# ScalarE's order written out for the whole kernel, and two roundings per block pair moved from ScalarE to GpSimd

## The chip, the core and the metric

The kernel runs on one core of a Trainium2 chip. The metric is the device time of one execution in microseconds. Five engines work side by side, each through its own queue in order: TensorE (PE in the profile, its weight loads PEld), VectorE (DVE), ScalarE (ACT), GpSimd (POOL) and SyncE (SP), which here only issues transfers. They wait for each other through semaphores.

## The reference

Two parts, one after the other. First an attention through 49 agents, for 4 batches of 12480 rows of 128 numbers:

```python
a2k = sm(agents, k)          # softmax over the 12480 rows of k
agent_v = a2k @ v            # 49 x 128 per batch
q2a = sm(q, agents)          # softmax over 49, for each row of q
x = q2a @ agent_v
h = x @ w_in                 # 128 -> 2048
out = (h - tanh(h)) @ w_out  # 2048 -> 128
```

`sm` scales by 1/sqrt(128), subtracts the maximum, exponentiates and divides by the sum. All is fp32, and `w_in` and `w_out` come as 64-bit floats that the kernel decodes.

## The kernel before

`agent_v @ w_in` is computed once per batch (49 x 2048), so that h comes straight from p, the softmax of q. Most products are made from fp32 numbers split in two, a rounded high part (fp32r) and the low rest; the two parts of p lie one above the other on 98 partitions, and the 49 x 2048 matrix is kept twice to match.

The main loop works on blocks of 500 columns (25 per batch, 100 in all). A block has 8 steps of 256 of the 2048 hidden units; two blocks make a pair of 16 steps (`pos` 0 to 15), and there are 50 pairs, 800 steps. For a step k the chain is:

- TensorE: h = two halves x two parts, four matmuls (`m1`, L544 and L545), into one of three PSUM buffers.
- ScalarE: y = tanh(c h) (L554), then z = y squared (L556). Both have two buffers. h times z is, up to a factor, h - tanh(h) for the small h that occur.
- VectorE: g = h z (`mul`, L562).
- GpSimd (or ScalarE): gh = g rounded (`high`, L595 on GpSimd, L593 on ScalarE).
- VectorE: gl = g - gh (`low`, L600).
- TensorE: six matmuls into the output block (`m2`): four with gh (L612, L613), two with gl (L615). One step in 16, and all of block 0, uses plain fp32 instead (L609) and has no gh or gl.

In iteration k of the loop TensorE makes h of step k+2 and then the output matmuls of step k-1; VectorE makes g of step k and then gl of step k-1; ScalarE makes y and z of step k+1.

Between these stand jobs, generators that advance by one stage in each iteration (`live`): the softmax of the next pair's q (`q_softmax`, begun at position 2: scores on TensorE L495, maximum on VectorE L502, a copy out of PSUM on ScalarE L503, the subtraction of the maximum on GpSimd L506, the exponential L510, sum and division L512 to L515, the rounded part of p on ScalarE L518, the low part on GpSimd L521); transposes of p and their copies (L531, L536); the copy of a finished output block (`finish`, o, L776). During the first three batches there is also work for the next batch: scores with k (three groups per pair, L278, L280, L286), then value products (three per pair, begun at positions 1, 3 and 12: subtraction on GpSimd L322, exponential L329, matmuls L337, sum L349), then the projection with `w_in` (L458 to L472).

What sets the order: on VectorE, GpSimd and TensorE each instruction has an ordering link to the one before it in program order (`issue_order`, L873 to L875). On ScalarE that holds only up to the eighth step (L860). After that a scheduler places ScalarE's instructions, with one rule: jobs of an iteration come behind the square of the iteration before (L840). `wait_for` (L635) adds a real wait: from the third pair on, the q subtraction and the low part of p wait until the latest `mul` is done. `QGAPS` says how many iterations lie between the stages of `q_softmax`; `QACT` names the two positions (4 and 9) whose rounding ScalarE does; in iterations that begin a value product ScalarE rounds too.

## Time and profile before

| | |
|---|---|
| three runs | 2145.88, 2146.28, 2146.33 us; median 2146.28 |
| profiled execution | 2144.79 us, span 2143.0 us, mean granted TensorE clock 0.997 |
| first and last product g | begin 59.0 us, end 2133.2 us |
| TensorE, VectorE, ScalarE, GpSimd busy | 2085.6, 1960.8, 1918.9, 1312.3 us |
| roundings on GpSimd, on ScalarE | 608, mean 1744 ns; 135, mean 1026 ns |
| VectorE's product waits for ScalarE's square | 134.7 us in 177 places |

A row of a timeline reads: start in us from the span's beginning, duration, engine, line, operation, what is written <- what is read, shapes, count; in brackets the engine's idle time before it and what ended that. TensorE's matmuls are pipelined and their ends modelled: one of 500 columns shows 0.39 us, while the next begins after about 0.23. A busy share near 100% therefore hides short stalls.

### The profile page before, as it was taken

To read this page: it belongs to the slowest core of one execution; us is meant where nothing else is said; L and a number is where in the kernel's file an instruction comes from. 1 tells how busy PE (TensorE), PEld (TensorE's weight loads), DVE (VectorE), ACT (ScalarE), POOL (GpSimd) and SP (SyncE) were. 2 spreads that over 40 slices of the span, in tenths; PEclk is the share of its full clock that TensorE was granted. 3 is DMA by queue.
4 is the path that set the end of the run, shared out by engine and by line. 5 is a ranking of instruction groups with operands and counts; after the bars stand their busy time and mean duration, and the time that the engine had idled before them with its cause. 6 is when DMAs were issued, how large, how long until landed. Compare 5 with 4: busy or idle time off the path is not lost.

```text
span 2143.0 us, 37562 instructions
## 1 busy us (share of the span) xinstructions
PE 2085.6 (97%) x14885; PEld 1632.7 (76%) x14885; DVE 1960.8 (91%) x2028; ACT 1918.9 (90%) x2232; POOL 1312.3 (61%) x761
## 2 busy tenths in 40 slices
PE   8999999999999999999999999999999999999998
PEld 7577777777777777777777777777777877777776
DVE  7899898989998999888999989998999999999998
ACT  3888899899998889989998889988999999999997
POOL 0465675556656665565666566655566766767666
PEclk9999999999999999999999999999999999999999
DMA  9222112210111111112002210121010010000000
GB/s 352 76 79 70 42 39 70 61 50 30 39 50 50 62 59 50 50 51 68 20 20 69 69 33 20 52 66 42 20 40 20 20 39 20 30 29 20 29 11 21
DMA packets 65353, 109.17 MB, mean 51 GB/s; under 512 B 3984, under 2 KB 44176, under 8 KB 65168
## 3 DMA queue, kind: packets, MB, share of 16 engines
q1 hardware_dynamic: 65168, 106.68, 15.2%
q8 instruction: 119, 1.95, 0.4%
q14 instruction: 66, 0.54, 0.1%
HBM read 81.10 MB, written 25.56 MB: 50 GB/s over the span
## 4 chain that ended last, share of the span: by engine, by line
PE 69%; DVE 16%; ACT 8%; issue 5%; DMA 1%; POOL 0%; SPq 0%; ACTq 0%; POOLq 0%; DVEq 0%
PE h L544 14%; PE misc L615 13%; PE h L545 13%; PE misc L612 11%; PE misc L613 11%; DVE gl L600 7%; DVE g L562 5%; ACT z L556 4%; PE misc L609 3%; ACT y L554 2%; PE misc L337 2%; PE misc L278 1%; PE misc L531 1%; PE h L250 1%; PE misc L495 1%
## 5 line engine op out<-in xcount | busy, mean ns | idle before, releaser
L595 POOL TENSOR_SCALAR gh<-g 128x1000 fp32r<-128x1000 f32 (+1 forms) x608 | 1060.6, 1744 | 663.9 <-DVE g L562 609.1
L562 DVE TENSOR_TENSOR g<-h,z 128x1000 f32<-128x1000 f32 (+1 forms) x800 | 951.8, 1192 | 144.4 <-ACT z L556 134.7
L600 DVE TENSOR_TENSOR gl<-g,gh 128x1000 fp32r<-128x1000 f32 (+1 forms) x743 | 906.4, 1220 | 9.5 <-ACT gh L593 4.8
L554 ACT ACTIVATE y<-h 128x1000 f32<-128x1000 f32 (+1 forms) x800 | 801.6, 1002 | 106.2 <-PE h L545 101.2
L556 ACT ACTIVATE z<-y 128x1000 f32<-128x1000 f32 (+1 forms) x800 | 828.0, 1040 | 19.5 <-DVE g L562 0.6
L544 PE MATMUL h<-pT,awh 98*128 98x500 f32 (+1 forms) x1600 | 670.2, 419 | 2.6 <-ACT awh L461 1.4
L545 PE MATMUL h<-pT,awl 98*128 98x500 f32 (+1 forms) x1600 | 622.4, 389 | 0.2 <-DVE awl L464 0.2
L612 PE MATMUL misc<-gh,wo_l 128*128 128x500 f32 (+1 forms) x1486 | 576.1, 388 | 0.5 <-POOL gh L595 0.3
L613 PE MATMUL misc<-gh,wo_h 128*128 128x500 f32 (+1 forms) x1486 | 575.6, 387 | 0.0
L615 PE MATMUL misc<-gl,wo_h 128*128 128x500 f32 (+1 forms) x1486 | 469.1, 397 | 37.6 <-DVE gl L600 35.6
L615 PEld LDWEIGHTS misc<-gl,wo_h 128*128 128x128 f32 x1486 | 265.8, 188 | 133.2 <-DVE gl L600 87.6
L544 PEld LDWEIGHTS h<-pT,awh 98*128 98x128 f32 x1600 | 300.7, 188 | 85.5 <-issue 15.2
L545 PEld LDWEIGHTS h<-pT,awl 98*128 98x128 f32 x1600 | 302.7, 189 | 65.9 <-issue 14.4
L612 PEld LDWEIGHTS misc<-gh,wo_l 128*128 128x128 f32 x1486 | 279.6, 188 | 57.9 <-POOL gh L595 1.9
L613 PEld LDWEIGHTS misc<-gh,wo_h 128*128 128x128 f32 x1486 | 280.7, 189 | 56.0
L593 ACT CAST gh<-g 128x1000 fp32r<-128x1000 f32 (+1 forms) x135 | 138.6, 1026 | 0.0
L506 POOL TENSOR_TENSOR qe<-qe,qm 126x392 f32<-126x392 f32 x50 | 81.6, 1631 | 83.5 <-ACT qe L503 42.3
L521 POOL TENSOR_TENSOR pp<-qe,pp 126x392 fp32r<-126x392 f32 x50 | 94.2, 1885 | 24.4 <-ACT pp L518 7.5
L322 POOL TENSOR_TENSOR s<-s,mb 128x392 f32<-128x392 f32 (+1 forms) x39 | 70.2, 1800 | 50.5 <-DVE g L562 50.5
L609 PE MATMUL misc<-g,wo_f 128*128 128x500 f32 (+1 forms) x196 | 90.1, 581 | 0.0
L536 ACT CAST pT<-misc 98x500 fp32r<-98x500 f32 (+1 forms) x100 | 56.1, 562 | 14.2 <-PE misc L531 14.2
L776 ACT ACTIVATE o<-misc 128x500 f32<-128x500 f32 (+1 forms) x100 | 57.2, 572 | 5.1 <-PE misc L615 5.1
(104 smaller groups left out, 838.3 us busy)
## 6 DMA issues: line engine op xcount, KB each, us to landing
kt<-kT SPq DMA_DIRECT2D x48, 512.0 KB, 3.8
qt<-qT SPq DMA_DIRECT2D x46, 500.0 KB, 3.6
outT<-o SPq DMA_DIRECT2D x46, 500.0 KB, 2.6
v<-v SPq DMA_DIRECT2D x36, 512.0 KB, 4.0
vt<-v SPq DMA_DIRECT2D x12, 512.0 KB, 7.5
raw<-w_in SPq DMA_DIRECT2D x4, 512.0 KB, 9.2
v<-w_out SPq DMA_DIRECT2D x4, 512.0 KB, 9.0
qt<-qT SPq DMA_DIRECT2D x4, 490.0 KB, 3.4
```

Of the source, the lines that this page charges most:

```text
L544: nc.tensor.matmul(h[:, c, :w], aw[0][:A2, sl], pT[:A2, :w], start=True, stop=False)
L545: nc.tensor.matmul(h[:, c, :w], aw[1][:A2, sl], pT[:A2, :w], start=False, stop=True)
L554: nc.scalar.activation(self.pair(y), h, AF.Tanh, scale=TSC)
L556: nc.scalar.activation(z, y, AF.Square)
L562: self.nc.vector.tensor_tensor(self.pair(g), h, self.pair(z), ALU.mult)
L593: self.nc.scalar.copy(gh, g)
L595: self.nc.gpsimd.tensor_scalar(gh, g, 1.0, 0.0, ALU.mult, ALU.add)
L600: self.nc.vector.tensor_tensor(gl, g, gh.bitcast(F32), ALU.subtract)
L609: nc.tensor.matmul(acc[:, :w], wf[:, c * C : (c + 1) * C], gh[:, x], start=f == 0, stop=f == NCH - 1)
L612: nc.tensor.matmul(acc[:, :w], self.wo_l[:, f, :], gh[:, x], start=f == 0, stop=False)
L613: nc.tensor.matmul(acc[:, :w], self.wo_h[:, f, :], gh[:, x], start=False, stop=False)
L615: nc.tensor.matmul(acc[:, :w], self.wo_h[:, f, :], gl[:, x], start=False, stop=f == NCH - 1)
```

## The change

- The constants: `QACT` is gone, `QGAPS` becomes (1, 1, 0, 2, 2, 1, 1). The q subtraction now comes in the same iteration as the copy before it (position 4 rather than 5), the exponential at position 6 rather than 7; sum and division stay at 8, the rounded p at 9, its low part at 10.
- The two waits for the latest `mul` in `q_softmax` are gone. That of the value product (L322) stays.
- `pre` is split in `tanh` and `square`. Iteration k now emits, for ScalarE: the tanh of step k+1, the jobs, a rounding if one is due, the square of step k+1.
- The roundings of positions 4 and 9 go to GpSimd. Only those of iterations that begin a value product stay on ScalarE, and they are emitted one iteration later, just ahead of the next square.
- ScalarE's order is fixed by links from end to end, as on the other engines.

The matmuls' order on TensorE and the transfers' on SyncE do not move, and VectorE's moves in one place only. No arithmetic is changed.

On ScalarE, around positions 8 to 11 of a pair with k scores, there stood before (o is the finished output block, s the scores, pp the split p, y, z, g, gh as above; numbers tell buffers apart):

```order
L518 CAST pp_2886<-qe_2703 126x8x49
L286 COPY s_1009<-misc_2813 128x392
L554 ACTIVATE y_2893<-h_2871 128x1000
L593 CAST gh_2899<-g_2897 128x1000
L556 ACTIVATE z_2895<-y_2893 128x1000
L776 ACTIVATE o_2910<-misc_2618 128x500
L554 ACTIVATE y_2918<-h_2888 128x1000
L554 ACTIVATE y_2939<-h_2913 128x1000
L556 ACTIVATE z_2920<-y_2918 128x1000
L556 ACTIVATE z_2941<-y_2939 128x1000
```

and now:

```order
L285 COPY s_1011<-misc_2815 128x392
L551 ACTIVATE z_2873<-y_2865 128x1000
L546 ACTIVATE y_2886<-h_2875 128x1000
L514 CAST pp_2888<-qe_2705 126x8x49
L551 ACTIVATE z_2890<-y_2886 128x1000
L546 ACTIVATE y_2910<-h_2892 128x1000
L770 ACTIVATE o_2912<-misc_2618 128x500
L551 ACTIVATE z_2915<-y_2910 128x1000
L546 ACTIVATE y_2934<-h_2917 128x1000
L551 ACTIVATE z_2936<-y_2934 128x1000
```

The rounding gh has left, the two tanh in a row have become one tanh and one square in turn, and the copies of s, p and o stand between a tanh and its square.

On GpSimd, in the same pair, from the rounding of position 3 on, before:

```order
L595 TENSOR_SCALAR gh_2692<-g_2690 128x1000
L506 TENSOR_TENSOR qe_2703<-qe_2703,qm_2702 126x392
L595 TENSOR_SCALAR gh_2776<-g_2774 128x1000
L595 TENSOR_SCALAR gh_2799<-g_2797 128x1000
L595 TENSOR_SCALAR gh_2882<-g_2880 128x1000
L521 TENSOR_TENSOR pp_2886<-qe_2703,pp_2886 126x8x49
L595 TENSOR_SCALAR gh_2924<-g_2922 128x1000
```

and now:

```order
L589 TENSOR_SCALAR gh_2692<-g_2690 128x1000
L504 TENSOR_TENSOR qe_2705<-qe_2705,qm_2704 126x392
L589 TENSOR_SCALAR gh_2719<-g_2717 128x1000
L589 TENSOR_SCALAR gh_2776<-g_2774 128x1000
L589 TENSOR_SCALAR gh_2800<-g_2798 128x1000
L589 TENSOR_SCALAR gh_2882<-g_2880 128x1000
L589 TENSOR_SCALAR gh_2899<-g_2897 128x1000
L516 TENSOR_TENSOR pp_2888<-qe_2705,pp_2888 126x8x49
L589 TENSOR_SCALAR gh_2924<-g_2922 128x1000
```

The rounding of position 4 (gh_2719) has come behind the q subtraction, that of position 9 (gh_2899) ahead of the low part of p.

On ScalarE, positions 3 to 6 of a pair with value products, before:

```order
L329 ACTIVATE s_1009<-s_1009 128x392
L593 CAST gh_4035<-g_4033 128x1000
L554 ACTIVATE y_4058<-h_4024 128x1000
L503 COPY qe_4049<-misc_3991 126x392
L556 ACTIVATE z_4060<-y_4058 128x1000
L554 ACTIVATE y_4089<-h_4053 128x1000
L593 CAST gh_4064<-g_4062 128x1000
L556 ACTIVATE z_4091<-y_4089 128x1000
L329 ACTIVATE s_1009<-s_1009 128x392
L554 ACTIVATE y_4112<-h_4084 128x1000
L556 ACTIVATE z_4114<-y_4112 128x1000
L510 ACTIVATE qe_4049<-qe_4049 126x392
```

and now:

```order
L546 ACTIVATE y_4045<-h_4028 128x1000
L328 ACTIVATE s_1011<-s_1011 128x392
L502 COPY qe_4049<-misc_3993 126x392
L587 CAST gh_4054<-g_4033 128x1000
L551 ACTIVATE z_4056<-y_4045 128x1000
L546 ACTIVATE y_4075<-h_4058 128x1000
L551 ACTIVATE z_4086<-y_4075 128x1000
L546 ACTIVATE y_4105<-h_4088 128x1000
L506 ACTIVATE qe_4049<-qe_4049 126x392
L328 ACTIVATE s_1011<-s_1011 128x392
L551 ACTIVATE z_4110<-y_4105 128x1000
```

The rounding of position 3 (of g_4033) has gone behind the next tanh, the exponential and the q copy; that of position 4 (gh_4064) has left; and the two exponentials of position 6 stand together ahead of a square.

```diff
-QGAPS = (1, 1, 1, 2, 1, 1, 1)
-QACT = (4, 9)
+QGAPS = (1, 1, 0, 2, 2, 1, 1)
...
         yield from (None,) * gaps[2]
-        first = self.count()
         nc.gpsimd.tensor_tensor(ev, ev, m[:TT, :, None].broadcast_to([TT, GT, A]), ALU.subtract)
-        if gaps != (1,) * 7:
-            self.wait_for(first, self.mul_at)
...
-        first = self.count()
         nc.gpsimd.tensor_tensor(pp[:TT, :, A:], ev, pp[:TT, :, :A].bitcast(F32), ALU.subtract)
-        if gaps != (1,) * 7:
-            self.wait_for(first, self.mul_at)
...
-    def pre(self, h, w):
-        nc = self.nc
+    def tanh(self, h, w):
         y = self.wtile("y", NB["y"])[:, : 2 * w]
-        nc.scalar.activation(self.pair(y), h, AF.Tanh, scale=TSC)
-        z = self.wtile("z", NB["z"])[:, : 2 * w]
-        nc.scalar.activation(z, y, AF.Square)
-        self.act_at = self.last_name()
+        self.nc.scalar.activation(self.pair(y), h, AF.Tanh, scale=TSC)
+        return y
+
+    def square(self, y):
+        z = self.wtile("z", NB["z"])[:, : y.shape[1]]
+        self.nc.scalar.activation(z, y, AF.Square)
         return z
...
+        def tanhs(k):
+            if k < len(steps):
+                ys[k] = self.tanh(hs[k], width(steps[k][0]))
+
         def squares(k):
+            for n, at in enumerate(r1):
+                if at[3] is ET.Activation:
+                    r1[n] = at[:3] + (self.high(at[2], True),)
             if k < len(steps):
-                zs[k] = self.pre(hs[k], width(steps[k][0]))
+                zs[k] = self.square(ys.pop(k))
...
-            gh = None if plain else self.high(g, act)
+            gh = None if plain else ET.Activation if act else self.high(g)
...
+        tanhs(0)
         squares(0)
...
-            first = self.count()
+            tanhs(k + 1)
             while done and done[0][1] < k - 1:
                 finish(done.pop(0)[0])
...
             live[:] = nxt
-            self.hold(first, self.act_at, (ET.Activation,))
+            squares(k + 1)
             first_product(k + AHEAD)
-            squares(k + 1)
             begin = kq and n and pos in kq[0][0]
             values = begin and kq[0][0] is VS
-            product(k, values or p and pos in QACT and p + 1 < npair)
+            product(k, values)
...
-            if n == 0 and i == HP - 1:
-                self.issue_order(ET.Activation, at)
...
         self.issue_order(ET.DVE, at)
+        self.issue_order(ET.Activation, at)
         self.issue_order(ET.Pool, early)
```

More of the change, by code (lines that the diff above doesn't have):

```diff
@@ L762, in fast @@
         r1, r2, done = [], [], []
-        acc, outs, hs, zs = {}, {}, {}, {}
+        acc, outs, hs, ys, zs = {}, {}, {}, {}, {}
         def start(gen):
```

## The prediction

> **What bounds the kernel now.** I read the page first: busy times, the chain that ended last, the costliest groups (busy time, mean ns of one, then idle time before them and who ended it).
>
> ```profile
> span 2143.0 us, 37562 instructions
> PE 2085.6 (97%) x14885; PEld 1632.7 (76%) x14885; DVE 1960.8 (91%) x2028; ACT 1918.9 (90%) x2232; POOL 1312.3 (61%) x761
> PE 69%; DVE 16%; ACT 8%; issue 5%; DMA 1%; POOL 0%; SPq 0%; ACTq 0%; POOLq 0%; DVEq 0%
> L595 POOL TENSOR_SCALAR gh<-g 128x1000 fp32r<-128x1000 f32 (+1 forms) x608 | 1060.6, 1744 | 663.9 <-DVE g L562 609.1
> L562 DVE TENSOR_TENSOR g<-h,z 128x1000 f32<-128x1000 f32 (+1 forms) x800 | 951.8, 1192 | 144.4 <-ACT z L556 134.7
> L600 DVE TENSOR_TENSOR gl<-g,gh 128x1000 fp32r<-128x1000 f32 (+1 forms) x743 | 906.4, 1220 | 9.5 <-ACT gh L593 4.8
> L593 ACT CAST gh<-g 128x1000 fp32r<-128x1000 f32 (+1 forms) x135 | 138.6, 1026 | 0.0
> ```
>
> TensorE is the bound, but VectorE (DVE) and ScalarE (ACT) each stand within a tenth of it. So a local delay on either can surface as a TensorE stall, because the last two matmuls of each step wait for gl. VectorE itself loses 134.7 us waiting for ScalarE's square (the row of L562). GpSimd (POOL) is idle for a third of the span. The waits say how VectorE's delays reach TensorE (total, times, longest):
>
> ```profile
> PEld misc L615 <- DVE gl L600: 87.6, 143, 1.7
> ```
>
> Next I looked at one pair (16 steps) of each kind. The columns are: stretch, its length, busy time of PE, PEld, DVE, ACT, POOL, then TensorE clock, DMA share, GB/s.
>
> ```profile
> 699.20:742.00 42.80, 41.82 (x424) 32.85 (x423) 38.48 (x40) 37.89 (x44) 26.83 (x16) 1.00 0.20 62
> 914.00:958.30 44.30, 42.66 (x280) 32.89 (x279) 39.33 (x40) 39.97 (x48) 25.16 (x16) 1.00 0.16 50
> 533.00:573.50 40.50, 40.09 (x236) 31.52 (x235) 38.96 (x41) 37.90 (x43) 26.66 (x16) 1.00 0.08 27
> 1943.00:1981.80 38.80, 38.75 (x232) 30.70 (x231) 36.83 (x37) 36.78 (x41) 26.90 (x16) 1.00 0.08 27
> ```
>
> They are a pair with k scores (K pair, about 12 in the run: 13 groups in each of three batches, three a pair), one with the value products (V pair, about 12), one with projections (P pair, about 6) and one of the last batch, where none of these run (plain pair, about 18 with the transitions). In the plain pair TensorE is idle 0.05 us, so nothing is to be had there. In K and V pairs it is idle 0.98 and 1.64 us, and no engine is full: there the order of the work costs time, and there the change can win.
>
> **The change, part by part.** I follow VectorE through a pair. Product k and gl(k-1) follow each other 1.11 us apart when nothing is waited for (product and gl at 1956.14 and 1957.25 below; one gl to the next 2.22, at 1966.72 and 1968.94). Whatever comes on top is a wait.
>
> *Step 10, two tanh ahead of two squares.* In a K pair:
>
> ```profile
> 726.16 1.04 ACT L556 ACTIVATE z<-y 128x1000 f32<-128x1000 f32 x1
> 727.10 0.58 ACT L776 ACTIVATE o<-misc 128x500 f32<-128x500 f32 x1
> 727.56 2.17 ACT L554 ACTIVATE y<-h 128x1000 f32<-128x1000 f32 x2
> 729.62 1.97 ACT L556 ACTIVATE z<-y 128x1000 f32<-128x1000 f32 x2
> 727.24 1.20 DVE L562 TENSOR_TENSOR g<-h,z 128x1000 f32<-128x1000 f32 x1 [1.00 <-ACT z L556]
> 730.69 1.20 DVE L562 TENSOR_TENSOR g<-h,z 128x1000 f32<-128x1000 f32 x1 [1.15 <-ACT z L556]
> 733.05 0.71 PE L615 MATMUL misc<-gl,wo_h 128*128 128x500 f32 x2 [0.92 <-DVE gl L600]
> ```
>
> The product at 727.24 waits 1.00 us, because the rounding that the change takes off ScalarE (1026 ns) lies before the square at 726.16. The one at 730.69 waits 1.15 us, because the second tanh lies before the first square. The new order has tanh, o, square, and no rounding. Both waits go: -2.2 us of VectorE's time in K pairs. V pairs show the same pattern; in a plain pair only 0.31 us waits here (1970.44 below).
>
> *The rounding of step 9 on GpSimd, and the low part of p behind it.* GpSimd's operations and gl exclude each other, and whichever starts first goes first:
>
> ```profile
> 920.65 1.03 POOL L595 TENSOR_SCALAR gh<-g 128x1000 fp32r<-128x1000 f32 x1 [1.11 <-DVE g L562]
> 920.68 2.04 DVE L600 TENSOR_TENSOR gl<-g,gh 128x1000 fp32r<-128x1000 f32 x1 [0.19 <-ACT gh L593]
> 1965.66 1.03 POOL L595 TENSOR_SCALAR gh<-g 128x1000 fp32r<-128x1000 f32 x1 [4.10 <-DVE g L562]
> 1966.72 1.20 DVE L600 TENSOR_TENSOR gl<-g,gh 128x1000 fp32r<-128x1000 f32 x1
> 1966.76 1.99 POOL L521 TENSOR_TENSOR pp<-qe,pp 126x392 fp32r<-126x392 f32 x1
> 1968.94 1.19 DVE L600 TENSOR_TENSOR gl<-g,gh 128x1000 fp32r<-128x1000 f32 x1
> 1969.19 1.84 POOL L595 TENSOR_SCALAR gh<-g 128x1000 fp32r<-128x1000 f32 x1 [0.44 <-DVE g L562]
> 1970.44 1.20 DVE L562 TENSOR_TENSOR g<-h,z 128x1000 f32<-128x1000 f32 x1 [0.31 <-ACT z L556]
> L521 POOL TENSOR_TENSOR pp<-qe,pp x50: 1133/1930/2026, 43.7 to 2083.0; 126x392 fp32r<-126x392 f32 x50
> ```
>
> A gl that finds GpSimd at work takes 2.04 us instead of 1.19, and ends 1.04 us after GpSimd does. A rounding begun behind a gl ends 2.09 us after that gl's start (1968.94 to 1971.03). Until now the wait for the product (L522) let pp's subtraction begin 0.04 us *behind* gl, where it cost nothing. Now count from the start of gl(8): the rounding of step 9 ends at about 2.07, pp's subtraction follows at once and, alone, takes 1.13 (the smallest of its 50), to 3.2. gl(9) is due at 2 x 1.11 = 2.22, finds GpSimd busy, and ends at 3.2 + 1.04 = 4.2 instead of 3.4: +0.8 us in every pair. The bounds are 0, if GpSimd starts 0.15 us later than I think, and +1.13. I take 0.8: even here, where pp's subtraction waited for the product, it came 0.07 us after the rounding before it (1965.66 + 1.03 to 1966.76). In the plain pair this replaces the wait of 0.31, which with its latency is 0.4: net +0.4.
>
> *The q subtraction in step 4, its rounding on GpSimd.*
>
> ```profile
> 1952.78 0.49 ACT L503 COPY qe<-misc 126x392 f32<-126x392 f32 x1 [0.76 <-DVE qm L502]
> 1953.24 1.01 ACT L554 ACTIVATE y<-h 128x1000 f32<-128x1000 f32 x1
> 1955.06 1.04 ACT L556 ACTIVATE z<-y 128x1000 f32<-128x1000 f32 x1
> 1956.14 1.20 DVE L562 TENSOR_TENSOR g<-h,z 128x1000 f32<-128x1000 f32 x1 [1.18 <-ACT z L556]
> 1957.25 1.19 DVE L600 TENSOR_TENSOR gl<-g,gh 128x1000 fp32r<-128x1000 f32 x1
> L506 POOL TENSOR_TENSOR qe<-qe,qm x50: 844/1661/1667, 35.1 to 2070.3; 126x392 f32<-126x392 f32 x50
> ```
>
> The copy filled a time in which ScalarE waited for TensorE anyway; now it follows the tanh at 1953.24, and the square follows the copy. Tanh, copy and square end at about 1953.24 + 0.91 + 0.41 + 1.04 = 1955.6, not 1956.10: -0.5 us. GpSimd can subtract from 1954.7; it is through by 1955.7 (0.84 to 0.95 us), rounds for 1.03 us, and gl(4) finds its operand ready at 1956.75, where VectorE is too. So -0.5 us here, with a rounding that comes just in time. In a K pair VectorE is 0.2 us nearer, which leaves -0.5 for the product and +0.2 for gl. The bounds are -1.18 (the whole wait) and +0.3, if the next rounding gets in ahead of gl(4) and costs 0.8.
>
> *Jobs between a tanh and its square.* This goes against the change. In a K pair:
>
> ```profile
> 716.94 0.48 ACT L286 COPY s<-misc 128x392 f32<-128x392 f32 x1
> 718.24 0.53 ACT L510 ACTIVATE qe<-qe 126x392 f32<-126x392 f32 x1
> 718.39 1.20 DVE L562 TENSOR_TENSOR g<-h,z 128x1000 f32<-128x1000 f32 x1
> ```
>
> Here the square ran between these two (717.30), and the product at 718.39 followed it. Now copy and exponential (moved from step 7 to step 6) both precede the square: +0.41 + 0.46, and with the earlier product +0.75 us. The copies of steps 1 and 8 stand likewise before a square; the one of step 8 waits on VectorE's maximum besides: +0.25 and +0.5 us. In a V pair ScalarE has more in one step:
>
> ```profile
> 924.50 0.52 ACT L329 ACTIVATE s<-s 128x392 f32<-128x392 f32 x1
> 925.88 0.99 ACT L554 ACTIVATE y<-h 128x1000 f32<-128x1000 f32 x1
> 927.51 1.19 DVE L600 TENSOR_TENSOR gl<-g,gh 128x1000 fp32r<-128x1000 f32 x1
> ```
>
> The rounding of step 3 stays on ScalarE, but behind the tanh at 925.88, the exponential and the q copy. From that tanh, which cannot start earlier by more than 0.1: 925.8 + 0.91 + 0.46 + 0.41 + 1.03 = 928.6, and gl(3), which began at 927.51, has to wait for it: +1.1 us at TensorE. Step 6 has two exponentials between tanh and square (+0.5 each), step 13 a pT copy and a rounding (+0.7).
>
> **The sum**, as VectorE's waits and as TensorE feels them.
> - K pair: step 1 +0.25, step 4 -0.5, step 6 +0.75, step 8 +0.5, step 10 -2.2, gl(4) and gl(9) +0.2 and +0.8, together -0.2, and some 0.5 less because a VectorE that is late at steps 8 to 10 finds done what it had waited for there: -0.7 for VectorE, of which TensorE gets 0.6. Times 12: -7 us. Bounds: 0 and -0.98 - 0.6 (its idle time and what its modelled ends hide): -19 to 0.
> - V pair: the gain of step 10 (-2.2 with gl(9)'s 0.8 taken off: -1.4) comes after +1.1 at step 3 and before +0.7 at step 13: about +0.5. Times 12: +6. Bounds -2.2 and +1.3: -26 to +16.
> - P pair: VectorE is its limit (38.96 of 40.50 busy) and waits for nothing at step 10, so gl(9)'s 0.8 shows, 0.6 at TensorE: +4 for 6. Bounds 0 to +5.
> - Plain pair: -0.5 and +0.4: about 0. Times 18: +1. Bounds -0.3 and +0.5 each: -5 to +9.
>
> Together +4 us on the profiled execution's 2144.8 us (span 2143.0 and 1.8 around it): 2149 us. The runs' median is 2146.28, 1.5 us over the profiled one, inside what I can resolve here. What moves is large (96 roundings, 98 us off ScalarE); what arrives is not, since ScalarE was only late at a few places, and two of them are paid back at the port.
>
> **The rivals.**
>
> *Faster.* gl(9) keeps its place, because GpSimd starts pp's subtraction 0.15 us later than its neighbours suggest, or ScalarE, 98 us lighter, runs far enough ahead to hide the jobs. For it: 134.7 us of waits for z. Against: pp's subtraction no longer waits for the product. Then K pairs get -1.3, V pairs -0.5, P pairs 0, plain pairs -0.3: -16 - 6 - 5 = -27, 2118; with half of it, 2130.
>
> *Slower.* GpSimd, now with a queue at steps 4 to 6, starts the next rounding ahead of a gl that waits for the last one. Each such case costs 0.8 us more (2.04 against 1.19). Its place is gl(3) to gl(5); it decides once GpSimd is through less than 0.05 us before gl can start. In my times K and V pairs lie that near, plain pairs 0.2 us off. K pairs hide it behind the late square of step 6; 12 V pairs and half of the other 24 pay: 24 x 0.8 = +19: 2168. The Trainium skill (SBUF — State Buffer, "Who interferes with whom") puts it as issue order deciding who blocks; the 2.04 us row agrees.
>
> *The moved roundings on the path.* If GpSimd's slower pace counted, 96 x (1744 - 1026) ns = +69 us, 2214. Against: it is idle 663.9 us ahead of its roundings. The Trainium skill (Trainium Kernel Development and Optimization, "Optimizing GPSIMD Operations") advises other engines where possible; by that rule the change would lose these 69 us.
>
> *Hidden anyway.* TensorE hides all of it: 2145 to 2147.
>
> **How the numbers follow.** The forecast 0.40, faster 0.26, slower 0.22, on the path 0.03, hidden 0.09. About 0.2% (4.3 us) can be told from no change: 2142.0 and 2150.6. The forecast, 2142 to 2157, puts 0.03 below, 0.22 inside and 0.15 above. Faster: 0.29; same: 0.31; slower: 0.40. The range 2122 to 2170 leaves out the best of the faster case and the worst of the slower.
>
> **What would show it.** Right: gl of about 2 us appear in step 10 of nearly every pair, some 50 in all, with pp's subtraction running at their start; ScalarE's two tanh in a row are gone; the product's waits for z come down from 134.7 only to 80 to 120 us; the K pair shrinks to about 42.2, V and P pairs grow by half a microsecond. Wrong: no long gl in step 10, and K and V pairs fall below 41.8 and 43.8 (faster), or roundings stand at the start of long gl in the plain pairs (slower).

## The result and the profile after

The changed kernel takes 2157.02 us (median of five, 2155.92 to 2158.08), the kernel before 2145.88 us in the same comparison (2144.15 to 2146.33): a ratio of 1.0053, interval 1.0038 to 1.0068. It is slower, by 11 us. The profiled execution took 2158.05 us, 13.3 us more than that of before, and the readings below account for these 13.3.

The page after: busy times, the chain that ended last, and the groups that answer to those shown of before (busy time, mean ns, idle time before and what ended it).

```profile
span 2156.3 us, 37634 instructions
PE 2093.9 (97%) x14885; PEld 1633.4 (76%) x14885; DVE 1980.1 (92%) x2028; ACT 1814.4 (84%) x2136; POOL 1387.0 (64%) x857
PE 58%; DVE 22%; ACT 8%; issue 7%; POOL 4%; DMA 0%; POOLq 0%; SPq 0%; DVEq 0%; ACTq 0%
L589 POOL TENSOR_SCALAR gh<-g 128x1000 fp32r<-128x1000 f32 (+1 forms) x704 | 1214.0, 1724 | 600.2 <-DVE g L556 513.5
L556 DVE TENSOR_TENSOR g<-h,z 128x1000 f32<-128x1000 f32 (+1 forms) x800 | 950.2, 1190 | 80.0 <-ACT z L551 74.4
L594 DVE TENSOR_TENSOR gl<-g,gh 128x1000 fp32r<-128x1000 f32 (+1 forms) x743 | 926.0, 1246 | 63.7 <-ACT gh L587 56.8
```

ScalarE lost 104.5 us of work (1918.9 to 1814.4) and 96 roundings went to GpSimd, as the change says. VectorE's waits for the square fell from 134.7 to 74.4 us. But a wait has come that hardly existed: gl for a rounding made by ScalarE, 56.8 us, where all of gl's waits had been 9.5. The chain shows the same: TensorE's share fell from 69% to 58%, VectorE's rose from 16% to 22%, GpSimd's from 0% to 4%. The waits of after (total, times, longest):

```profile
ACT y L546 <- PE h L538: 267.0, 439, 3.6
DVE gl L594 <- ACT gh L587: 56.8, 39, 1.7
PEld misc L606 <- ACT gh L587: 29.1, 39, 1.0
PE misc L606 <- ACT gh L587: 12.6, 39, 0.6
```

and the first of these rows as it was before:

```profile
ACT y L554 <- PE h L545: 101.2, 243, 1.5
```

There are 39 such roundings, three in each of the twelve pairs full of value products (V pairs) and one in each of three pairs at the borders, and each of the 39 is waited for, by gl and by TensorE itself. ScalarE at the same time waits longer for TensorE, 267.0 us instead of 101.2: it is not short of time, its work stands in the wrong order.

The same four kinds of pair as in the prediction, with the same columns (stretch, length, PE, PEld, DVE, ACT, POOL): with k scores (K), V, with projections (P), plain.

```profile
704.60:746.40 41.80, 41.49 (x423) 32.79 (x423) 39.04 (x39) 35.20 (x43) 28.17 (x18) 1.00 0.20 64
920.76:966.20 45.44, 43.43 (x280) 32.77 (x279) 38.92 (x39) 38.46 (x46) 26.55 (x18) 1.00 0.16 49
539.10:580.10 41.00, 40.29 (x235) 31.35 (x234) 39.75 (x40) 35.22 (x42) 28.28 (x18) 1.00 0.08 26
1956.30:1995.00 38.70, 38.49 (x231) 30.84 (x231) 37.47 (x37) 34.56 (x40) 28.55 (x18) 1.00 0.08 28
```

Mean lengths of a pair, worked out from the starts of the products (first product of a pair to that of the next); the nine others are the first, the last, and those at the borders of the kinds:

| us | K (12) | V (12) | P (6) | plain (11) | nine others together |
|---|---|---|---|---|---|
| before | 42.68 | 44.16 | 40.35 | 38.75 | 363.7 |
| after | 41.81 | 45.53 | 40.93 | 38.69 | 367.6 |
| difference in all | -10.4 | +16.5 | +3.5 | -0.7 | +3.9 |

That makes 12.8 of the 13.3 us; the rest lies before the first product and behind the last. The V pairs alone lose more than the whole kernel does. Some 1.5 of their 16.5 us happened only once: in the first V pair of this profile (46.94 us, the other eleven 45.40 on average) the granted TensorE clock is 0.66 from 331 to 336 us, and no other profile here shows such a dip inside the main loop. What set it off is not shown.

What a late rounding looks like, positions 3 and 4 of one V pair on the timeline (start, duration, engine; in brackets the idle time ahead and what ended it):

```profile
929.42 1.19 DVE L556 TENSOR_TENSOR g<-h,z 128x1000 f32<-128x1000 f32 x1
...
935.00 2.01 DVE L594 TENSOR_TENSOR gl<-g,gh 128x1000 fp32r<-128x1000 f32 x1 [1.70 <-ACT gh L587]
930.14 1.04 ACT L551 ACTIVATE z<-y 128x1000 f32<-128x1000 f32 x1
932.24 1.01 ACT L546 ACTIVATE y<-h 128x1000 f32<-128x1000 f32 x1 [1.06 <-PE h L538]
933.15 0.52 ACT L328 ACTIVATE s<-s 128x392 f32<-128x392 f32 x1
933.56 0.48 ACT L502 COPY qe<-misc 126x392 f32<-126x392 f32 x1
933.93 1.04 ACT L587 CAST gh<-g 128x1000 fp32r<-128x1000 f32 x1
934.93 1.04 POOL L589 TENSOR_SCALAR gh<-g 128x1000 fp32r<-128x1000 f32 x1
```

The g to be rounded is there at 930.61. ScalarE has ended a square at 931.18 and then stands idle for 1.06 us, with the rounding ready to run: its queue goes in order, and the next in it is a tanh that waits for TensorE's h. Behind that tanh come the exponential and the q copy, and only at 933.93 the rounding. VectorE waits 1.70 us for it. And the delay brings a second one: GpSimd's next rounding has started 0.07 us ahead of gl, so gl takes 2.01 us instead of 1.19.

### The profile page after: what moved, and what is told of

It is laid out like the page before. It is cut to its first block, busy times and chain, and to the rows that moved or that the text cites. A ratio compares the mean times of both kernels' runs of the same rounds, so it can differ in the third digit from the quotient of the medians.

```text
span 2156.3 us, 37634 instructions
## 1 busy us (share of the span) xinstructions
PE 2093.9 (97%) x14885; PEld 1633.4 (76%) x14885; DVE 1980.1 (92%) x2028; ACT 1814.4 (84%) x2136; POOL 1387.0 (64%) x857
## 4 chain that ended last, share of the span: by engine, by line
PE 58%; DVE 22%; ACT 8%; issue 7%; POOL 4%; DMA 0%; POOLq 0%; SPq 0%; DVEq 0%; ACTq 0%
PE h L537 12%; PE misc L609 11%; DVE gl L594 11%; PE h L538 11%; PE misc L606 8%; PE misc L607 8%; DVE g L556 8%; POOL gh L589 3%; ACT z L551 2%; PE misc L336 2%; ACT gh L587 2%; PE misc L603 1%; ACT y L546 1%; PE misc L494 1%; PE h L249 1%
## 5 line engine op out<-in xcount | busy, mean ns | idle before, releaser
L589 POOL TENSOR_SCALAR gh<-g 128x1000 fp32r<-128x1000 f32 (+1 forms) x704 | 1214.0, 1724 | 600.2 <-DVE g L556 513.5
L546 ACT ACTIVATE y<-h 128x1000 f32<-128x1000 f32 (+1 forms) x800 | 805.9, 1007 | 270.5 <-PE h L538 267.0
L556 DVE TENSOR_TENSOR g<-h,z 128x1000 f32<-128x1000 f32 (+1 forms) x800 | 950.2, 1190 | 80.0 <-ACT z L551 74.4
L594 DVE TENSOR_TENSOR gl<-g,gh 128x1000 fp32r<-128x1000 f32 (+1 forms) x743 | 926.0, 1246 | 63.7 <-ACT gh L587 56.8
L606 PE MATMUL misc<-gh,wo_l 128*128 128x500 f32 (+1 forms) x1486 | 580.3, 390 | 13.1 <-ACT gh L587 12.6
L606 PEld LDWEIGHTS misc<-gh,wo_l 128*128 128x128 f32 x1486 | 279.6, 188 | 85.7 <-ACT gh L587 29.1
L504 POOL TENSOR_TENSOR qe<-qe,qm 126x392 f32<-126x392 f32 x50 | 52.5, 1050 | 111.4 <-ACT qe L502 111.4
L603 PEld LDWEIGHTS misc<-g,wo_f 128*128 128x128 f32 x196 | 37.0, 189 | 26.3 <-issue 22.6
L516 POOL TENSOR_TENSOR pp<-qe,pp 126x392 fp32r<-126x392 f32 x50 | 49.3, 985 | 7.5 <-ACT pp L514 7.5
```

Source lines behind the costliest of these rows:

```text
L546: self.nc.scalar.activation(self.pair(y), h, AF.Tanh, scale=TSC)
L556: self.nc.vector.tensor_tensor(self.pair(g), h, self.pair(z), ALU.mult)
L589: self.nc.gpsimd.tensor_scalar(gh, g, 1.0, 0.0, ALU.mult, ALU.add)
L594: self.nc.vector.tensor_tensor(gl, g, gh.bitcast(F32), ALU.subtract)
L603: nc.tensor.matmul(acc[:, :w], wf[:, c * C : (c + 1) * C], gh[:, x], start=f == 0, stop=f == NCH - 1)
L606: nc.tensor.matmul(acc[:, :w], self.wo_l[:, f, :], gh[:, x], start=f == 0, stop=False)
```

## The experiments

Three theories stood against each other. Theory A is the one just read: the roundings that stay on ScalarE and are emitted one iteration later, behind a tanh, make the loss. Against it stood that the low part of p, now ahead of gl at position 10, costs it (rival B, the collision of the prediction), and that the jobs between a tanh and its square do (rival C). All ratios are to the kernel before, with their intervals. The mean lengths of pairs are of one profiled execution each, counted as in the table above.

**e1: the ScalarE roundings early again.** They are emitted straight behind the square, ahead of the next tanh; all else is as after.

```diff
         def squares(k):
-            for n, at in enumerate(r1):
-                if at[3] is ET.Activation:
-                    r1[n] = at[:3] + (self.high(at[2], True),)
...
-            gh = None if plain else ET.Activation if act else self.high(g)
+            gh = None if plain else self.high(g, act)
```

> The changed kernel, with ScalarE's rounding of a value-product step put right behind the square that goes before it (ahead of the next tanh, as soon as the product can be there), not one iteration later. Theory A (the late rounding makes gl wait, and that is what the change loses in V pairs): the waits of gl for ScalarE's rounding, 56.8 us in 39 places, fall below 15 us; the product after the next waits up to 0.9 us for its square instead; V pairs come from 45.5 us to 43.8-44.6; the run to 2138-2147. Rival B (the GpSimd port at steps 4 and 10 is what it loses): V pairs stay above 45.2, the run at 2153-2158. Rival C (jobs between tanh and square): the same as B.

Measured: 2109.91 us, ratio 0.9831 (0.9815 to 0.9847). The V pair of e1 as a stretch:

```profile
895.89:937.72 41.83, 41.83 (x280) 33.29 (x279) 38.19 (x40) 38.11 (x46) 28.50 (x18) 1.00 0.17 53
```

And the same place on its timeline:

```profile
904.09 1.20 DVE L556 TENSOR_TENSOR g<-h,z 128x1000 f32<-128x1000 f32 x1 [0.91 <-ACT z L551]
...
907.90 1.19 DVE L594 TENSOR_TENSOR gl<-g,gh 128x1000 fp32r<-128x1000 f32 x1
904.98 1.04 ACT L551 ACTIVATE z<-y 128x1000 f32<-128x1000 f32 x1
905.93 1.01 ACT L587 CAST gh<-g 128x1000 fp32r<-128x1000 f32 x1
906.85 1.00 ACT L546 ACTIVATE y<-h 128x1000 f32<-128x1000 f32 x1
```

The same rounding, of the same length, now fills what was idle time, gl follows without a wait, and the V pair goes from 45.53 to 41.80 us, with no idle time of TensorE shown. K, P and plain pairs are as in after, to 0.02 us. So the lateness of three roundings costs 3.7 us a V pair (3.6 without the pair of the low clock): with the borders between the kinds, 47 of after's 2157 us. Theory A holds, and its effect is several times what I had expected of this run. VectorE still waits here (0.91 us for the square above), and TensorE does not feel it.

**e2: these roundings on GpSimd instead.** `product(k, values)` becomes `product(k, False)`.

> The changed kernel with no rounding on ScalarE at all: the three of a V pair go to GpSimd too. A: no wait of gl for ScalarE is left, gl pays for the value subtraction at the port instead, some 0.6 us in three places; V pairs 43.5-44.8 us, the run 2136-2149. B: with three more roundings on GpSimd the port gets worse, V pairs 45.5 or more, the run 2156-2170. C: V pairs lose what the two exponentials of step 6 cost and no more, 45 or so, the run 2150-2156. K, P and plain pairs stay as in the changed kernel (41.8, 40.9, 38.7).

Measured: 2110.83 us, 0.9839 (0.9823 to 0.9856). V pairs 41.85 us, like e1. Both runs come out far below what was expected of them. Which engine rounds makes no difference in this order; that it rounds in time does. The cost is small: the s subtraction runs into a gl at step 13 in nine V pairs (some 0.65 us each) and makes the two others 0.2 to 0.3 us longer in all twelve, and TensorE does not show it.

**e3: ScalarE's new order, with everything else of q as before.** The gaps, the roundings of positions 4 and 9 on ScalarE (by the new rule also emitted late) and the two waits are back.

```diff
-QGAPS = (1, 1, 0, 2, 2, 1, 1)
+QGAPS = (1, 1, 1, 2, 1, 1, 1)
+QACT = (4, 9)
...
+        first = self.count()
         nc.gpsimd.tensor_tensor(ev, ev, m[:TT, :, None].broadcast_to([TT, GT, A]), ALU.subtract)
+        if gaps != (1,) * 7:
+            self.wait_for(first, self.mul_at)
...
-            product(k, values)
+            product(k, values or p and pos in QACT and p + 1 < npair)
```

> Only ScalarE's written-out order, with the old q job: the q subtraction and the low part of p wait for the product again, in their old steps, and ScalarE rounds at positions 4 and 9 (behind the next tanh, as it does in V pairs). A: the late rounding now costs some 1.3 us at positions 4 and 9 of every pair: plain pairs 38.7 to 39.5-40.5, V pairs 46 and more, the run 2180-2220. B: without the collision of the low part of p with gl every pair gains about 0.6 us on the changed kernel; plain pairs 38.7 or less, P pairs 40.3, the run 2125-2145. C: as the changed kernel, 2150-2160, since the jobs stand where they stood in it.

Measured: 2187.29 us, 1.0194 (1.0177 to 1.0211). There are 135 late roundings now, and the wait's row counts almost all of them (x127, 123.2 us):

```profile
DVE gl L601 <- ACT gh L594: 123.2, 127, 1.7
```

A plain pair, which had no late rounding in after, takes 40.12 us instead of 38.69. So the loss is not bound to V pairs: a late rounding costs time in a plain pair too. It does not show alike in every kind: K pairs take 42.45 us (41.81 in after) and P pairs 40.90 (40.93). In both, two late roundings have come, but the long gl of position 10 are gone as well (one K pair excepted), so a gain may hide part of the loss.

**e4: the other half alone.** The kernel before with the new gaps, without the two waits, and with the roundings of positions 4 and 9 on GpSimd; ScalarE's order is the scheduler's.

```diff
-QGAPS = (1, 1, 1, 2, 1, 1, 1)
-QACT = (4, 9)
+QGAPS = (1, 1, 0, 2, 2, 1, 1)
...
-        if gaps != (1,) * 7:
-            self.wait_for(first, self.mul_at)
...
-            product(k, values or p and pos in QACT and p + 1 < npair)
+            product(k, values)
```

> Only the q job's part of the change: the roundings of positions 4 and 9 on GpSimd, the new steps, no waits for the product; ScalarE's order left to the scheduler of the kernel before, which then puts jobs ahead of a tanh, and each V rounding ahead of the square. A: V pairs lose no more than 0.3 us on the kernel before (44.2) and may gain; K pairs gain as in the changed kernel (41.5-42), since the two tanh in a row are gone here too; P pairs lose 0.6 at the port; the run 2130-2143. B: gl of about 2 us in step 10 of 47 pairs as in the changed kernel, and the run no faster than it, 2150-2160. C: K pairs about 1 us better than the changed kernel's 41.8 (step 7's 0.83 us of wait is gone), the run 2125-2140.

Measured: 2112.8 us, 0.9848 (0.9832 to 0.9865), better than expected. K 41.23, V 43.24, P 40.20, plain 38.50 us: every kind gains, though the collision at position 10 is there in P, V and plain pairs. The change thus has a half that wins 33 us and a half, the written order with its late roundings, that takes 44 away. The lateness alone makes up that loss: e1 has the written order too, with the roundings early, and at 2109.91 us it is no slower than e4 (V pairs shorter, the other kinds longer).

**e5: the jobs ahead of the tanh.** From e2; tanh and square of a step stand together again.

```diff
-            tanhs(k + 1)
             while done and done[0][1] < k - 1:
...
             live[:] = nxt
+            tanhs(k + 1)
             squares(k + 1)
```

> The changed kernel without any rounding on ScalarE, and with the jobs of an iteration ahead of its tanh (jobs, tanh, square) where the change has them between the two. If the place of the jobs costs what I put on it (rival C, second to the late rounding): the product's waits for its square at steps 5, 7 and 9 shrink, K pairs from 41.8 to 41.1-41.4, P pairs from 40.9 to 40.2-40.5, V pairs from 41.9 to 41.0-41.6, the run 2085-2100. If jobs ahead of a tanh only move the wait to the tanh (the h it reads has long been there): K, P and V pairs within 0.2 us of what they were, the run 2107-2113.

Measured: 2107.51 us, 0.9822 (0.9805 to 0.9838), 3 us under e2, though the two intervals overlap. In time this is the second case of the expectation; by kind it is neither. P pairs fall by 0.73 and plain pairs by 0.19 us, but K pairs rise from 41.82 to 42.16. Why, at position 8 of a K pair:

```profile
711.19 0.56 DVE L279 TENSOR_REDUCE s<-misc 128x49 f32<-128x392 f32 x1
...
714.27 1.20 DVE L556 TENSOR_TENSOR g<-h,z 128x1000 f32<-128x1000 f32 x1 [1.42 <-ACT z L551]
...
711.78 0.49 ACT L285 COPY s<-misc 128x392 f32<-128x392 f32 x1 [2.11 <-DVE s L279]
712.16 1.01 ACT L546 ACTIVATE y<-h 128x1000 f32<-128x1000 f32 x1
```

The s copy waits for VectorE's maximum, 2.11 us, and the tanh stands behind it. That is the same fault as the late rounding, seen from the other side: work that could run is queued behind work that cannot.

**e6, e7, e8: the q stages one step closer,** so that the low part of p comes at position 8, which has no gl to collide with. `QGAPS = (1, 1, 0, 1, 1, 1, 1)`, on e2 (e6), on e5 (e7), and on e1 with the jobs ahead of the tanh (e8).

> The changed kernel without any rounding on ScalarE, and with the q job's stages one step closer: exponential in step 5, sums in step 6, p in step 7, its low part in step 8, where one block in two has no rounding and no gl of step 7, so that GpSimd stands idle. If the collision of the low part of p with gl costs what it shows (rival B, 47 gl of 1.7 to 1.9 us in step 10): those are gone, VectorE gains 0.6 us a pair, TensorE 0.3-0.6 in P and V pairs and 0.1-0.4 in K and plain pairs, the run 2085-2103. If TensorE hid it: the long gl are gone and the run is at 2107-2113 all the same.

> Both: no rounding on ScalarE, jobs ahead of the tanh, the q job's stages one step closer. If both costs are real and apart from each other, the gains add: 2065-2085; K 40.8-41.2, V 40.8-41.3, P 39.8-40.2, plain 38.2-38.5. If they hide behind the same TensorE time: no better than the better of the two alone, 2085-2100.

> As the kernel with both, but the rounding of a value-product step on ScalarE, right behind the square before it. The late rounding being the only harm in having it on ScalarE (theory A), it is as good as on GpSimd: V pairs within 0.4 us of the kernel with both, the run within 5 us of it. If ScalarE's 1.03 us itself is too much in those steps: V pairs 0.5-1.5 us longer, the run 6-18 us longer.

Measured: 2140.7 us, 0.9978 (0.9969 to 0.9988); 2136.13 us, 0.9956 (0.9942 to 0.997); 2135.68 us, 0.9954 (0.9937 to 0.9971): 26 to 30 us over e1, e2 and e5. In K, V and plain pairs the collision only moved, to gl(6), and a plain pair takes about 40 us (40.28, 39.89 and 39.88). Positions 6 to 8 of one in e6:

```profile
1947.73 0.55 DVE L508 TENSOR_REDUCE qs<-qe 126x8 f32<-126x392 f32 x1
...
1949.00 0.57 DVE L511 TENSOR_TENSOR qe<-qe,qs 126x392 f32<-126x392 f32 x1
1949.48 1.19 DVE L556 TENSOR_TENSOR g<-h,z 128x1000 f32<-128x1000 f32 x1
...
1952.81 1.84 DVE L594 TENSOR_TENSOR gl<-g,gh 128x1000 fp32r<-128x1000 f32 x1
...
1952.64 0.95 POOL L516 TENSOR_TENSOR pp<-qe,pp 126x392 fp32r<-126x392 f32 x1
...
1951.84 0.72 PE L609 MATMUL misc<-gl,wo_h 128*128 128x500 f32 x2 [1.19 <-DVE gl L594]
```

Sum, division and product of the softmax hold VectorE from 1947.73 to 1949.5. At position 8, where they stood before, a gl is missing (the step is the one in plain fp32) and they fill its place; two positions earlier they come on top, TensorE stalls 1.19 us for gl, and with VectorE late, p's subtraction starts 0.17 us ahead of the next gl all the same. I had moved the collision and not asked what else moves with the stages. That the moved softmax does this is read from one pair, and no run parts it from the collision: in P pairs, where the collision did go, e6 takes 40.49 us against e2's 40.94, but the softmax moved there too. So these runs do not say what the collision costs. They do say once more that an early rounding on ScalarE is as good as one on GpSimd: V pairs take 42.86 us in e8 and 42.84 in e7.

**e9: e4 with all roundings on GpSimd,** `product(k, False)`: no rounding is left on ScalarE for the scheduler to place.

> The q job's part of the change with ScalarE's order left to the scheduler, and in V pairs no rounding on ScalarE either. If the rounding on ScalarE is what keeps V pairs of that kernel at 43.2 us: V pairs come to 41.3-41.9, the other kinds stay (41.2, 40.2, 38.5), the run 2092-2100. If V pairs are held there by their exponentials and copies ahead of the tanh: V pairs 42.5-43.3, the run 2103-2113.

Measured: 2097.47 us, 0.9771 (0.9755 to 0.9788): 2.3% under the kernel before, the best of all that compute the same. The page, then a K, a V, a P and a plain pair:

```profile
span 2096.1 us, 37705 instructions
PE 2070.0 (99%) x14885; PEld 1643.3 (78%) x14885; DVE 1996.9 (95%) x2028; ACT 1834.9 (88%) x2097; POOL 1459.5 (70%) x896
PE 77%; DVE 14%; ACT 5%; issue 2%; DMA 1%; POOL 1%; SPq 0%; POOLq 0%; DVEq 0%; ACTq 0%
```

```profile
683.80:725.05 41.25, 41.25 (x424) 32.98 (x423) 39.09 (x40) 36.85 (x42) 28.81 (x18) 1.00 0.21 65
891.05:932.90 41.85, 41.85 (x280) 33.31 (x279) 39.69 (x40) 36.64 (x43) 30.85 (x21) 1.00 0.17 53
520.80:561.15 40.35, 40.07 (x236) 31.45 (x235) 39.93 (x40) 36.57 (x41) 28.81 (x18) 1.00 0.08 27
1896.90:1935.40 38.50, 38.46 (x232) 30.82 (x231) 37.80 (x36) 35.56 (x39) 29.10 (x18) 1.00 0.08 27
```

In K and V pairs TensorE shows no idle time, and its share of the chain is 77%. GpSimd has 147 us more to do than in the kernel before (1459.5 against 1312.3) and is 1% of the chain.

**e10: e5 with the s copy one iteration later** (a `yield` between the maximum and `nc.scalar.copy(st["s"]...)`).

> The kernel with jobs ahead of the tanh, the copy of the k scores one iteration after the maximum it waits for. If that copy, waiting for VectorE ahead of a tanh, is what leaves K pairs at 42.2 us there (the product's wait of 1.38 us in step 9): the wait goes, K pairs 41.0-41.4, the run 2093-2099. If K pairs are held by the collision of step 10 or by TensorE: K pairs 41.8 or more, the run 2103-2108.

Measured: 2105.77 us, 0.9809 (0.9793 to 0.9825). The wait at position 9 falls from 1.38 to 0.13 us, as expected, but the K pair only from 42.16 to 41.88, about where e2 had it (41.82): new waits of 0.49 us (a square) and 0.19 us (q's maximum, for TensorE) appear at position 3. The scheduler's K pair (41.23) was not reached.

**e11: e2 without the low part of p,** which takes the collision away and nothing else of the order. The copy writes the rounded p into both halves, so what the kernel computes is no longer the reference's result; it serves to price the collision. The copy itself takes 0.84 us instead of 0.52.

```diff
-        nc.scalar.copy(pp[:TT, :, :A], ev)
+        nc.scalar.copy(pp[:TT].rearrange("p t (two a) -> p t two a", two=2), ev[:, :, None, :].broadcast_to([TT, GT, 2, A]))
-        nc.gpsimd.tensor_tensor(pp[:TT, :, A:], ev, pp[:TT, :, :A].bitcast(F32), ALU.subtract)
```

> The changed kernel without any rounding on ScalarE, and without GpSimd's subtraction for the low part of p: ScalarE writes the rounded p into both halves instead, some 0.3 us more for it, so the result is that of a p counted twice. It takes the collision in step 10 away and leaves the order as it is. If the collision costs what I predicted (0.6 us at TensorE in P pairs, less elsewhere): P pairs from 40.9 to 40.3, K and V pairs 0.1-0.6 shorter, the run 2090-2103. If TensorE hides it and the P pairs' loss comes from the jobs between tanh and square: all kinds within 0.15 us, the run 2106-2113.

Measured: 2092.79 us, 0.975 (0.9734 to 0.9766), 18 us under e2. By kind: P 40.94 to 40.32, plain 38.69 to 38.20, K 41.82 to 41.56, V 41.85 to 41.81. The collision is real and TensorE feels it, 0.5 to 0.6 us in the pairs where VectorE is near full (P and plain). But in P pairs it is not a price by itself. A P pair in e2, in e5 and in e11, one row from each kernel:

```profile
521.40:562.50 41.10, 40.38 (x235) 31.43 (x235) 39.81 (x41) 35.26 (x42) 28.33 (x18) 1.00 0.08 26
```

```profile
523.70:564.10 40.40, 40.12 (x236) 31.50 (x235) 39.97 (x41) 36.57 (x41) 28.86 (x18) 1.00 0.08 27
```

```profile
519.20:559.65 40.45, 40.06 (x235) 31.49 (x235) 39.16 (x41) 35.51 (x42) 27.35 (x17) 1.00 0.08 27
```

e5 has the collision, six long gl at position 10 in its six P pairs, as in e2, and they are as short as without it. Either edit gives the 0.6 to 0.7 us back, so the two delays, jobs ahead of the square and the collision, seem to use up one slack between them. No run leaves out both; what is left to gain beyond either is at most the idle time that TensorE shows in these rows, 0.28 and 0.39 us, and what its modelled ends hide. In plain pairs it is otherwise: e5, with the collision, takes 38.50 us and e11 38.20, so at least 0.3 us stay with the collision when the jobs are out of the way. e9 has the same collisions in its P, V and plain pairs.

**e12: e9 with one rounding of the pairs without k or v work back on ScalarE** (position 9; in all 20) and p's subtraction waiting for the product again, so that it comes behind gl.

```diff
+        if gaps != (1,) * 7:
+            self.wait_for(first, self.mul_at)
...
-            product(k, False)
+            product(k, p and pos == 9 and p + 1 < npair and not (kq and kq[0][0] in (KS, VS)))
```

> The fastest kernel so far (the q job's new steps, the scheduler's order on ScalarE, no rounding of V steps there), with the rounding of step 9 given back to ScalarE in the 20 pairs that have neither scores nor value products, and the low part of p waiting for the product again, so that it goes behind gl there as in the kernel before. If the collision is worth what the run without that subtraction gave (0.5 us in plain, 0.6 in P pairs) and ScalarE has 1.03 us to spare in those pairs: long gl of step 10 left in V pairs only, plain pairs 38.0-38.3, the run 2086-2092. If ScalarE's rounding there costs as much again (the product's wait of 0.3 us at step 11 in the kernel before): plain pairs 38.4-38.7, the run 2094-2100.

Measured: 2100.88 us, 0.979 (0.9776 to 0.9803), not better than e9. A P pair takes 40.60 us instead of 40.20, a plain pair 38.62 instead of 38.51: gl at position 10 waits for ScalarE's rounding (0.28 us on average in P pairs), and in five of six P pairs another rounding is ahead of it. In plain pairs the long gl of position 10 are gone, but the product of step 11 now waits 0.74 us for its square. In these pairs something as dear took the collision's place.

## Why the prediction was right in its time, and where its sum was not

It said 2149 us, 2122 to 2170, slower the likeliest by a little; it is 2157.0. The four terms of its sum, forecast against measured: K pairs -7 and -10.4 us, P pairs +4 and +3.5, plain pairs +1 (with the borders) and -0.7 with +3.9 at the borders and ends, V pairs +6 and **+16.5**. The term that was mis-sized is the V pairs: it is as large as the upper bound that the prediction gave it. That the time still lies near the forecast is partly luck, since the K pairs came out 3 us better than their term; and of the forecast +4 us its author had said that it could not be told from no change.

**K pairs: right in the direction of every step.** VectorE's mean waits in the twelve K pairs, before and after, worked out from the trace; the first column names the step whose product or gl waits.

| place in the program | forecast | before | after |
|---|---|---|---|
| product behind the q copy (step 5) | -0.5 | 1.15 | 0.47 |
| product behind two jobs (step 7) | +0.75 | under 0.1 | 0.83 |
| product behind the s copy (step 9) | +0.5 | under 0.1 | 0.35 |
| products behind two tanh (steps 10, 11) | -2.2 | 2.03 | under 0.1 |
| gl behind p's low part (step 10), longer by | +0.8 | 0 | 0.6 |
| product of step 2 | +0.25 | 0.36 | 0.41 |

The six differences measured add up to -0.88 us, and the pairs shrank by 0.87, to 41.8 us; the forecast was -0.7 for VectorE, 0.6 of it for the pair, and about 42.2. Its lump of -0.5 (a late VectorE finds done what it had waited for) is no row of its own: it shows in the entries that came out lower than forecast, at steps 5, 9, 2 and at gl.

**The collision: right in place and size, wrong as a price of its own.** Forecast: pp's subtraction gets ahead of gl(9) in nearly every pair, some 50 long gl, +0.8 us each. Measured: 47 pairs, gl of 1.70 to 1.87 us in most, 0.62 us over its 1.19 on average. One of them:

```profile
951.48 1.70 DVE L594 TENSOR_TENSOR gl<-g,gh 128x1000 fp32r<-128x1000 f32 x1
...
951.16 0.96 POOL L516 TENSOR_TENSOR pp<-qe,pp 126x392 fp32r<-126x392 f32 x1
952.09 1.99 POOL L589 TENSOR_SCALAR gh<-g 128x1000 fp32r<-128x1000 f32 x1
```

The subtraction took 0.96 us alone, less than the smallest of before (1.13), which accounts for most of the difference. The step "so gl(9)'s 0.8 shows, 0.6 at TensorE" for the P pair came out to the tenth (40.35 to 40.93), but partly by luck: the P term left out that the product of step 5 waits 0.69 us less there (1.16 to 0.47), and that VectorE waits a new 0.27 us for ScalarE's copy of awh (L460, a job that now stands between tanh and square). And e5 shows that the 0.6 needs the jobs between tanh and square too. The prediction had weighed the two apart.

**V pairs: three errors that partly cancel.** The forecast was -1.4 (position 10, net), +1.1 (the rounding of step 3), +0.7 (that of step 13): about +0.5.
- It counted two of the three late roundings, and these two too low. A V pair begins value products at positions 1, 3 and 12. The waits of gl are 1.38 us at step 2 (0.19 before; no term), 1.70 at step 4 (forecast 1.1) and 1.35 at step 13 (0.7): 4.2 us more, against the 1.8 in the sum. For step 4 the reason shows: the prediction let the tanh ahead of the rounding start where it had started before, 0.53 us ahead of the product of that step; it now waits 1.07 us for TensorE's h and starts 0.13 us behind that product (means of the twelve V pairs; the second is 932.24 on the timeline above). Besides, the late gl of step 4 finds GpSimd at work in all twelve V pairs, +0.82. This is the mechanism of the "slower" rival, at the place it names; it said that 12 V pairs and half of 24 others pay, and only the V pairs do, since elsewhere no gl is late there.
- The two exponentials at step 6, "+0.5 each", did not get into the sum: 1.18 at step 7.
- It left out what the same move frees. With the rounding gone from its old place, the product of step 3 no longer waits (1.00 before), and the gl of steps 2 and 5 no longer meet GpSimd (0.85 and 0.76 before).

Together: +4.2 + 0.8 + 1.2 - 2.4 (the products at steps 10 and 11) + 0.5 (gl at step 10) - 1.0 - 1.6 - 0.4 (smaller ones) = +1.3 us, against a measured +1.37 a pair. And one thing is not in this sum at all, since the prediction followed VectorE only: TensorE waits for the late gh itself, in its first four output matmuls (29.1 and 12.6 us in the rows above). What the late roundings are worth at the end of the pair is not 4.2 + 0.8: making them early gives 3.7 us a V pair back in e1, where other waits have come, of VectorE's product for its square.

**What was to show it.** Long gl in position 10 of some 50 pairs: 47. The two tanh in a row gone: yes. Waits for z at 80 to 120 us: 74.4, just below. V and P pairs up by half a microsecond: P yes, V 1.4. K pairs at about 42.2: 41.8. Roundings at the start of long gl in plain pairs, the sign of the slower rival: none.

**What the prediction ruled out.** It held that nothing is to be had in a plain pair, where TensorE shows 0.05 us of idle time. It takes 38.75 us before, 38.51 in e9 and 38.20 in e11, with the same matmuls: the 0.05 us hid that much.

**The other rivals.** "The moved roundings on the path", 2214 us: excluded. e4 moves them and is 33 us faster; e9 moves 39 more and gains another 15, and GpSimd's share of the chain, 4% in after, is 1% there. By the Trainium skill (Perfetto Trace Analysis, "Optimizing GPSIMD Operations"; the prediction names another page for this section), which advises other engines where possible, both should have lost. Here the measurement decides: GpSimd stood idle for 600.2 us ahead of its roundings, and ScalarE stands in the chain from TensorE to VectorE. A rounding that starts ahead of gl takes GpSimd 1.04 us (at 934.93 above), as long as ScalarE's (at 933.93); the longer mean, 1724 ns, holds its waits for VectorE. "Hidden anyway": excluded by the interval. "Faster", 2118 to 2130: after is not, but the half of it that moves the q work alone is (2112.8), with gl(9) losing its place in P, V and plain pairs. Its second reason, a ScalarE that is lighter by 98 us, fits e4 and e9, though no run parts the moved roundings from the new gaps; the late roundings of the written order kept the gain from showing.

## What to carry to other kernels

On an engine whose queue goes in order, ask of each instruction that others wait for: what stands ahead of it, and what does that wait for? A rounding of 1 us cost some 1.2 us at each of three places in a pair (3.7 us by e1) only because it was queued behind a tanh and other jobs that it could have run ahead of; at one of the three it was ready, and its engine idle, while the tanh waited for TensorE. And when a change has two halves, price and run them apart: here a gain of 33 us and a loss of 44 showed as a loss of 11.

## What the runs showed of the hardware that I had not expected

- When GpSimd has its next instruction ready, it still lets a waiting gl in first. In after 48 of the 50 low parts of p had a gl start 0.15 to 0.77 us behind them; that gl ended 1.02 to 1.06 us behind the subtraction, and GpSimd's next rounding, which follows the subtraction without a gap in all 48, ended 0.86 to 0.91 us behind the gl (952.09 + 1.99 = 954.08 above, against 953.18). So in these cases a gl lost one of GpSimd's instructions and no more. Whether the two take turns or go in the order in which they came is not shown, since in all 48 the gl stood waiting first.
- How much of VectorE's delay TensorE hides depends on where it falls. A product 0.91 us late shows no cost in the V pairs of e1 (41.80 us, and 41.85 in e2 without that wait). Of two delays of 0.5 and 0.65 us in a P pair either can be taken away, and 0.6 to 0.7 us are gained by it (e2, e5, e11). A count of waits in a view of groups does not tell these apart; leaving one out on the chip does.
